# Swapping two early loads, and laying block 1's inputs out in SBUF, in a fused transformer kernel

## The chip, the cores and the metric

The kernel runs on one core of a Trainium2 chip. The metric is the time of one execution on the device in microseconds (us). A kernel is executed several times, and medians are quoted. The profile is taken from one execution; its span, from the first to the last instruction, is about 1.8 us shorter than the time of the same execution.

Names used throughout: x0, x1, x2 are the first tiles of 128 rows of the input (256 KB each). q0 to q3 are the quarters of the weight w1 (512 KB each). PE is the tensor engine, DVE the vector engine, ACT the scalar engine, POOL the GpSimd engine, SP the engine whose queue issues most loads. PT is a tile of transposed probabilities in the attention blocks.

## The reference

Two branches read the same normalised input, and their sum is added to x.

```python
xn = _layernorm(x)
return x + _A_ref(xn, mem0, Wq, Wk, Wv, Wo, seg_len) + _B_ref(xn, w1, w2, w3, w4)

def _B_ref(x, w1, w2, w3, w4):            # x is 2048 x 1024
    h = _gelu(_layernorm(x) @ w1)         # the stage that starts the kernel
    hs = shifted_quarters(h) @ w2
    x1 = x + hs
    return x1 + _gelu(_layernorm(x1) @ w3) @ w4     # inner width 3584

def _A_ref(x, mem0, Wq, Wk, Wv, Wo, seg_len):
    # 64 segments of 32 rows with 8 memory rows, 32 heads of 128:
    # q, k, v, masked softmax, output product; memory goes from segment to segment
    ...
```

## The kernel before

Everything is in bfloat16 with accumulation in float32. The kernel runs branch B first, then all values of branch A (the "V phase"), then branch A's queries, keys, scores and outputs in five blocks of segments ("block 0" to "block 4").

The loads at the start all go through SP's queue:

```python
load_x(0)
load_x(1)
for c in range(4):
    nc.sync.dma_start(w1_sb[:, 2 * c:2 * c + 2, :], w1_v[:, 2 * c:2 * c + 2, :])
    if c == 1:
        load_x(2)
for n in range(3, 7):
    load_x(n)
# ... then w2 and further x tiles
```

The statistics and transposes of the first tiles, and the first product. `stage1_k` does tile 0 one w1 quarter at a time (two values of `k` each), so that PE can start when q0 has landed; `tr(1, ...)` are the transposes of tile 1, which need its normalised rows:

```python
norm_stats(0)
norm_stats(1, 0)          # half of tile 1's statistics
norm2_of(0)               # normalise tile 0
tr(0, 0, True); tr(0, 1, True)
norm_stats(1, 1)          # the other half
...
def stage1_k(xn2T):
    ...
    for k in range(KT):                   # KT = 8
        if k == KT - 2:
            tr(1, 0)
            tr(1, 1)
        for co in range(KT):
            nc.tensor.matmul(...)         # w1_sb[:, k, ...] times tile 0
```

In the V phase the inputs of the blocks are gathered from xT. Those of block 0 stay in SBUF; those of blocks 1 to 4 go through a staging tile to DRAM, and are fetched a block ahead of their use:

```python
if 1 <= hg < 5:
    b, (tl, nb) = hg, tiles_of(hg)
    hTs = abig.tile([P, KT, 464 if b > 2 else 416], BF16, tag="oX", name=f"hTs{b}")
    nc.gpsimd.memset(hTs[:], 0.0)
    fill(hTs, tl, lambda j, b=b: xT[:, j])          # DVE copies
    nc.gpsimd.dma_start(hT_d[b][:], hTs[:].rearrange("p k c -> p (k c)"))
...
if hg == 0:
    tl, nb = tiles_of(0)
    hTb0 = early.tile([P, KT, 416], BF16, tag="hTb0")
    fill(hTb0, tl, lambda j: xT[:, j])
```

```python
def block_setup(b):
    ...
    if b == 0:
        hTb = hTb0
    else:
        hTb = early.tile([P, KT, 464 if b > 2 else 416], BF16, tag=f"hTb{b % 2}")
        nc.gpsimd.dma_start(hTb[:].rearrange("p k c -> p (k c)"), hT_d[b][:])
```

## Time and profile before

| Reading | Before |
|---|---|
| median time, first three runs | 1512.88 us (1511.96 to 1513.14) |
| span of the profile | 1511.0 us |
| PE busy | 1499.8 us, 99% |
| PE waiting, where a cause is named | 3.6 us |
| tile 1's own matmuls begin | 13.57 us |

The page gives the span and the busy time of each engine, with the number of instructions.

```profile
span 1511.0 us, 24305 instructions
...
PE 1499.8 (99%) x9778; PEld 804.0 (53%) x9850; DVE 544.6 (36%) x1136; ACT 504.6 (33%) x1144; POOL 178.9 (12%) x248
```

The kernel is bound by PE nearly everywhere. What can be won by moving loads must therefore be found in PE's waits. The waits view of PE lists who waited for whom: total us, number of times, longest.

```profile
PE ps L307 <- DMA w_sb<-in_B_w_dram: 1.7, 3, 1.0
PE warm L334 <- DVE wz L328: 1.4, 1, 1.4
PE psO L694 <- DMA PT<-Pn: 0.5, 1, 0.5
```

The first line is the start: three waits for quarters of w1. The timeline of PE at the start shows them one by one (start, duration, line, operation, count, and in brackets the idle time just before with its releaser). L307 is tile 0's product, 16 matmuls to a quarter; L294 the transposes; L317 the product of tile 1.

```profile
7.96 1.07 PE L307 MATMUL ps<-xn2T,w_sb 128*128 128x128 bf16 x16 [0.47 <-DMA w_sb<-in_B_w_dram]
9.28 1.07 PE L307 MATMUL ps<-xn2T,w_sb 128*128 128x128 bf16 x16 [0.26 <-DMA w_sb<-in_B_w_dram]
11.32 1.07 PE L307 MATMUL ps<-xn2T,w_sb 128*128 128x128 bf16 x16 [0.97 <-DMA w_sb<-in_B_w_dram]
12.23 0.61 PE L294 MATMUL ps<-c_ident_sb,xn 128*128 128x128 bf16 x8
12.67 1.06 PE L307 MATMUL ps<-xn2T,w_sb 128*128 128x128 bf16 x16
13.57 2.84 PE L317 MATMUL ps<-xn2T,w_sb 128*128 128x128 bf16 x48
```

PE waits for q0, q1 and q2, and from 11.32 us on it is busy. The chain of work that ended last says the same in its first pieces (start, duration, what):

```profile
3.16 8.12 DMA w_sb<-in_B_w_dram
11.28 0.05 issue
11.32 1.07 PE ps L307 x16
```

The landing of q2 is thus the last thing at the start that is not PE's own work. The last two columns of the windows view are the mean busy share of the DMA engines and the rate in GB/s.

```profile
2.00:3.50 1.50, 1.50 (x5) 0.45 (x4) 0.07 (x1) 0.24 (x2) 0.61 (x1) 1.00 0.90 324
3.50:6.50 3.00, 3.00 (x8) 0.87 (x6) 2.69 (x7) 0.00 (x0) 0.72 (x1) 1.00 0.80 226
6.50:9.00 2.50, 2.03 (x25) 1.67 (x24) 1.61 (x5) 1.20 (x4) 1.02 (x4) 1.00 1.05 397
```

There is a dip from 3.5 to 6.5 us: 226 GB/s, against 397 afterwards. For the second half of the change, the same view over the V phase (its third to seventh columns are PE, weight loads, DVE, ACT and POOL), and the loads of block inputs out of DRAM in the view of the tile (count, durations of the issuing instruction in ns, first and last start):

```profile
535.00:756.00 221.00, 219.90 (x1004) 100.14 (x1024) 50.99 (x108) 38.31 (x65) 26.69 (x24) 1.00 0.52 179
```

```profile
L637 POOL DMA_DIRECT2D hTb<-hT_scratch x4: 534/537/558, 646.9 to 1196.1; - x4
```

PE is busy 219.9 of 221 us there; DVE and POOL have ample room. Block 1's load is the one issued at 646.9 us; block 1 itself begins near 870 us.

### The profile page before, as it was taken

What the parts mean: (1) busy time and instruction counts of PE and PEld (TensorE: products, weight loads), DVE (VectorE), ACT (ScalarE), POOL (GpSimd) and SP (SyncE); (2) the same over time, 40 slices, a digit from 0 to 9 for tenths busy, and PEclk for the clock granted to TensorE, in tenths of its full rate; (3) what the DMA queues carried; (4) which work ended last, traced back from release to release, by engine and by line L of the source; (5) the groups of instructions that cost most, each with busy time, mean ns of one, the idle gap of its engine ahead of it and who ended that gap; (6) DMA issues with size and microseconds to landing.
All of it is one profiled execution on the core that took longest, in us unless ns stands there. A gap on an engine that the chain in (4) does not pass through costs nothing.

```text
span 1511.0 us, 24305 instructions
## 1 busy us (share of the span) xinstructions
PE 1499.8 (99%) x9778; PEld 804.0 (53%) x9850; DVE 544.6 (36%) x1136; ACT 504.6 (33%) x1144; POOL 178.9 (12%) x248
## 2 busy tenths in 40 slices
PE   9999999999999999999999999999999999999998
PEld 7844444445444444444456645664665455545555
DVE  8383230100020122222246624661564166516641
ACT  6533203013012011111156614650663266416630
POOL 5231020211111231100000000001000100010001
PEclk9999999999999999999999999999999999999999
DMA  8699752453345887632389957992998299918811
GB/s 292 150 265 315 228 168 89 146 202 104 137 149 151 203 261 258 218 121 82 128 216 257 244 128 171 245 252 69 245 243 206 71 227 224 219 60 199 216 49 51
DMA packets 303539, 274.11 MB, mean 181 GB/s; under 512 B 153926, under 2 KB 270184, under 8 KB 303424
## 3 DMA queue, kind: packets, MB, share of 16 engines
q1 hardware_dynamic: 281248, 189.92, 50.1%
q0 software_dynamic: 22032, 82.54, 15.9%
q8 instruction: 79, 1.29, 0.4%
q14 instruction: 36, 0.29, 0.1%
q10 hardware_dynamic: 144, 0.07, 0.0%
HBM read 190.93 MB, written 46.14 MB: 157 GB/s over the span
## 4 chain that ended last, share of the span: by engine, by line
PE 98%; DMA 1%; issue 0%; SPq 0%; DVE 0%
PE ps L655 30%; PE pso L713 15%; PE ps L594 15%; PE ps L536 13%; PE ps L562 13%; PE ps L394 4%; PE ps L317 3%; PE psO L694 2%; PE psS L670 2%; PE ps L849 1%; PE ps L486 1%; DMA w_sb<-in_B_w_dram 1%; DMA PT<-Pn 1%; PE gps L465 0%; PE ps L451 0%
## 5 line engine op out<-in xcount | busy, mean ns | idle before, releaser
L655 PE MATMUL ps<-hTb,wt 128*128 128x396 bf16 (+2 forms) x2528 | 495.9, 343 | 0.0
L655 PEld LDWEIGHTS <-wt 128*128 128x128 bf16 x2528 | 232.7, 98 | 164.9 <-DMA wt<-in_A_Wq_dram 0.4
L594 PE MATMUL ps<-wt,xT 128*128 128x512 bf16 x1003 | 220.1, 379 | 1.1
L713 PE MATMUL pso<-wo_sb,oX 128*128 128x512 bf16 (+1 forms) x972 | 209.1, 372 | 1.1
L536 PE MATMUL ps<-xn3T,w_sb 128*128 128x512 bf16 x896 | 196.2, 379 | 0.0
L562 PE MATMUL ps<-w_sb,h3T 128*128 128x512 bf16 x873 | 194.3, 379 | 1.2
L594 PEld LDWEIGHTS <-xT 128*128 128x128 bf16 x1024 | 100.1, 98 | 120.9
L537 ACT ACTIVATE h3T<-ps 128x512 bf16<-128x512 f32 x112 | 66.8, 597 | 290.4 <-PE ps L536 289.5
L713 PEld LDWEIGHTS <-oX 128*128 128x128 bf16 x992 | 96.0, 98 | 106.6
L657 ACT CAST KT<-ps 128x462 bf16<-128x462 f32 (+2 forms) x160 | 81.7, 511 | 190.0 <-PE ps L655 185.9
L562 PEld LDWEIGHTS <-h3T 128*128 128x128 bf16 x896 | 86.9, 98 | 103.4
L536 PEld LDWEIGHTS <-w_sb 128*128 128x128 bf16 x896 | 86.5, 98 | 102.1
L676 DVE TENSOR_REDUCE sums<-sm 99x4 f32<-99x396 f32 (+2 forms) x176 | 97.6, 555 | 112.9 <-ACT sm L674 112.9
L659 ACT ACTIVATE QT<-ps 128x462 bf16<-128x462 f32 (+2 forms) x160 | 83.8, 524 | 112.6 <-PE ps L655 98.7
L596 ACT CAST Vs<-ps 128x512 bf16<-128x512 f32 x64 | 37.4, 585 | 233.2 <-PE ps L594 175.0
L672 DVE TENSOR_TENSOR sm<-psS,c_mask_reg_sb 99x396 f32<-99x396 f32 x152 | 86.7, 570 | 74.6 <-PE psS L670 74.5
L674 ACT ACTIVATE sm<-sm 99x396 f32<-99x396 f32 (+2 forms) x176 | 92.7, 527 | 57.7 <-DVE sm L672 53.5
L600 DVE CAST Vs<-ps 128x512 bf16<-128x512 f32 x64 | 44.3, 692 | 170.0 <-PE ps L594 160.4
L682 DVE TENSOR_TENSOR Pn<-sm,rs 99x396 bf16<-99x396 f32 (+2 forms) x176 | 98.9, 562 | 7.2 <-DMA PT<-Pn 1.1
L720 POOL DMA_DIRECT2D out_dram<-ot x30 | 16.4, 545 | 699.4 <-DVE ot L719 693.5
L563 DVE TENSOR_TENSOR R<-ps,R 128x512 f32<-128x512 f32 x32 | 21.9, 690 | 180.1 <-PE ps L562 166.2
L719 DVE TENSOR_TENSOR ot<-pso,Rt 128x512 bf16<-128x512 f32 (+1 forms) x33 | 22.2, 675 | 168.5 <-PE pso L713 164.5
(122 smaller groups left out, 1063.0 us busy)
## 6 DMA issues: line engine op xcount, KB each, us to landing
wt<-in_A_Wq_dram SPq DMA_DIRECT2D x76, 512.0 KB
wt<-in_A_Wk_dram SPq DMA_DIRECT2D x76, 512.0 KB
wt<-in_A_Wv_dram POOLq DMA_DIRECT2D x24, 1024.0 KB, 6.9
V_scratch<-Vs SPq DMA_DIRECT2D x32, 512.0 KB
V<-V_scratch SPq DMA_DIRECT2D x40, 384.0 KB
R_scratch<-x POOLq DMA_DIRECT2D x16, 512.0 KB, 4.0
R<-R_scratch SPq DMA_DIRECT2D x16, 512.0 KB
R_scratch<-R POOLq DMA_DIRECT2D x16, 512.0 KB, 3.1
```

The source lines that it names most:

```text
L536: nc.tensor.matmul(ps[:].rearrange("p (n t) -> p n t", t=P), w3_sb[:, k, f * P:(f + 1) * P], xn3T[tb][:, :, k, :], start=(k == 0), stop=(k ...
L537: nc.scalar.activation(h3T[:, f, :], ps[:], ACTF.Gelu_apprx_tanh)
L562: nc.tensor.matmul(ps[:], h3T[:, f, j * P:(j + 1) * P], w4_sb[:, f, ch * 512:(ch + 1) * 512], start=(f == 0), stop=(f == FT - 1))
L594: nc.tensor.matmul(ps[:], xT[:, m4 * 4 + j, k, :], wv[:, k, :], start=(k == 0), stop=(k == KT - 1))
L655: nc.tensor.matmul(ps[:, :nb], w[:, k, hh * P:(hh + 1) * P], B["hT"][:, k, :nb], start=(k == 0), stop=(k == KT - 1))
L657: nc.scalar.copy(dst[:, hh, :], ps[:, :nb])
L659: nc.scalar.mul(dst[:, hh, :], ps[:, :nb], scale)
L672: nc.vector.tensor_tensor(sm[:T, :, :T], S3, t["mask"][:].unsqueeze(1).to_broadcast((T, 4, T)), op=ALU.add)
L674: nc.scalar.activation(e[:T, :, :T], sm[:T, :, :T], ACTF.Exp, scale=LN2)
L676: nc.vector.tensor_reduce(ss, e[:T, :, :T], axis=AX.X, op=ALU.add)
L682: nc.vector.tensor_tensor(Pn[:T, :, :T], e[:T, :, :T], rs[:T, :].unsqueeze(2).to_broadcast((T, 4, T)), op=ALU.mult)
L713: nc.tensor.matmul(self.ps[:, :self.w], self.oX[0][:, h, self.oX[1] + self.gl * P:self.oX[1] + (self.gl + 1) * P], wo_sb[:, h, self.cc], s ...
```

## The change

Its intent: let PE start on q0 earlier by loading x1 behind q0 rather than ahead of it, and save block 1's inputs the way through DRAM. The place of x2 does not change: it was behind q1 before, and still is. The statistics of tile 1 are no longer cut in halves around tile 0's normalisation.

```diff
                     load_x(0)
-                    load_x(1)
                     for c in range(4):
                         nc.sync.dma_start(w1_sb[:, 2 * c:2 * c + 2, :], w1_v[:, 2 * c:2 * c + 2, :])
-                        if c == 1:
-                            load_x(2)
+                        if c < 2:
+                            load_x(1 + c)
@@
                     norm_stats(0)
-                    norm_stats(1, 0)
                     norm2_of(0)
                     tr(0, 0, True)
                     tr(0, 1, True)
-                    norm_stats(1, 1)
+                    norm_stats(1)
@@
-                if 1 <= hg < 5:
+                if hg < 2:
+                    tl, nb = tiles_of(hg)
+                    hTb01.append(early.tile([P, KT, 416 + 48 * hg], BF16, tag=f"hTb{hg}", name=f"hTb{hg}"))
+                    fill(hTb01[hg], tl, lambda j: xT[:, j])
+                elif hg < 5:
                     b, (tl, nb) = hg, tiles_of(hg)
@@
-            if b == 0:
-                hTb = hTb0
+            if b < 2:
+                hTb = hTb01[b]
             else:
                 hTb = early.tile([P, KT, 464 if b > 2 else 416], BF16, tag=f"hTb{b % 2}")
```

More of the change, by code (lines that the diff above doesn't have):

```diff
@@ L112 @@
     xn_v = xn_d.rearrange("(n p) d -> p n d", p=P)
-    hT_d = {b: tc.dram_tile([P, KT * c], BF16, name=f"hT{b}_scratch") for b, c in ((1, 416), (2, 416), (3, 464), (4, 464))}
+    hT_d = {b: tc.dram_tile([P, KT * c], BF16, name=f"hT{b}_scratch") for b, c in ((2, 416), (3, 464), (4, 464))}
     V_d = tc.dram_tile([S, H * DH], BF16, name="V_scratch")
@@ L580 @@
             wo_sb = abig.tile([P, H, D], BF16)
+            hTb01 = []
             pns = [abig.tile([112, 4, P], BF16, name=f"Pn{i}") for i in range(3)]
@@ L618 @@
                         nc.sync.dma_start(w[:], src[:, :, 512:1024])
-                if hg == 0:
-                    tl, nb = tiles_of(0)
-                    hTb0 = early.tile([P, KT, 416], BF16, tag="hTb0")
-                    fill(hTb0, tl, lambda j: xT[:, j])
             vctx.close()
```

## The prediction

> **What bounds the kernel.** The tensor engine. The page gives PE 1499.8 us busy of a 1511.0 us span (99%), clock 1.000; the chain that ended last is 98% PE. The waits view names 3.6 us of PE waiting: 1.4 at the start (a memset), 1.7 for w1's quarters (three waits, longest 1.0), 0.5 for one PT transpose at 799.4 us. The last 3.8 us (timeline) are the final eviction and store; the other idle time is scattered and looks like missing matmul records. Some 2 us lie where the change could act.
>
> **Part 1, the load order at the start.** Before: x0, x1, q0, q1, x2, q2, q3 on SP's queue (q = quarters of w1). After: x0, q0, x1, q1, x2, q2, q3. x1 (256 KB) and q0 (512 KB) swap; x2 keeps its place. In the timeline, PE starts q0's matmuls at 7.96 (0.47 waiting), q1's at 9.28 (0.26), q2's at 11.32 (0.97), q3's without waiting, and is busy from there; the chain has w1's DMA from 3.16 to 11.28, then only PE.
>
> The Trainium skill ("DMA: Bandwidth & Descriptors", Queues, rings and completion order) says that descriptors on an engine's ring are consumed in order. The trace agrees: these transfers are seen in order of issue. So q0 lands earlier by x1's share: 256 KB at about 390 GB/s (windows, 8 to 11 us), an estimated 0.7 us. PE can use 0.47 of it, as tile 0's transposes end at 7.49. But the bytes ahead of q1 and q2 are the same, so q1 still comes at about 9.28 and q2 at about 11.32; the 0.47 us becomes a longer wait before q1 (about 0.7). Gain on the chain: about 0.
>
> Cost: x1 lands later, near 8.0. Its statistics (twice 0.69, 0.21, 0.22), POOL's power (0.72) and the normalisation (0.55) then give tile 1's rows at about 11.0 instead of 9.3; PE transposes them at 12.2, so about 1 us of slack remains. x2's statistics follow later by 1 to 1.5 us, still before x3 comes (13.3). No loss either.
>
> **Part 2, block 1's inputs.** Removed: one POOL memset (2.90 us), one 832 KB store (about 4 us to landing), one 832 KB load (8.4 us, issued at 646.9). The DVE copies, under 2 us, stay. None is on the chain: the load lands some 200 us before block 1 starts; no PE wait for it is listed. In the V phase (535 to 756 us) PE waits for nothing named, and DVE's evictions wait for PE (2.8 us before each). PE's and ACT's instruction orders are unchanged. Gain: 0 to 0.2 us.
>
> **Prediction.** 1512.4 us, range 1510.8 to 1514.0; before was 1512.88. Chance of faster by over 2% 0.005, within 2% 0.99, slower 0.005. The sum is about -0.2; the other -0.3 is for the PT wait and the DMA dip.
>
> **What would show it.** Right: PE's first w1 matmul near 7.5; q1's wait grown; q2's matmuls still at 11.2 to 11.4; tile 1's transposes without a wait; PE busy within 1 us of 1499.8; three hT stores and loads instead of four. Wrong: q2's matmuls over 0.4 us earlier or later; a new PE wait for tile 1's rows; PE gaps vanishing between 535 and 756 us.
>
> **What would make it wrong.** DMA throughput dips from 3.5 to 6.5 us (139 to 287 GB/s, against 377 before and 410 after; windows). If it depends on the transfers in flight, the swap may move q2 by half a microsecond. A later DMA wait, such as PT's, may also shift.

## The result, and the profile after

| | Before | After |
|---|---|---|
| median of 6 runs each | 1513.01 us (1511.96 to 1513.98) | 1511.46 us (1511.15 to 1512.63) |
| span of the profile | 1511.0 us | 1509.4 us |
| tile 1's own matmuls begin | 13.57 us | 12.03 us |

The ratio is 0.9992, with a 95% interval of 0.9979 to 1.0005. (A ratio is the mean time of one kernel's fast runs over that of the other's of the same rounds, so it is not quite the ratio of the medians quoted.) The page after:

```profile
span 1509.4 us, 24295 instructions
...
PE 1498.9 (99%) x9778; PEld 804.2 (53%) x9850; DVE 544.8 (36%) x1136; ACT 505.2 (33%) x1144; POOL 175.4 (12%) x245
```

POOL is 3.5 us less busy, which is mostly the removed memset. PE's waits after:

```profile
PE warm L333 <- DVE wz L327: 1.4, 1, 1.4
PE psO L693 <- DMA PT<-Pn: 0.6, 2, 0.3
PE ps L306 <- DMA w_sb<-in_B_w_dram: 0.4, 1, 0.4
PE ps L293 <- DVE xn L274: 0.4, 1, 0.4
```

The waits for w1 fell from 1.7 to 0.4 us. PE's timeline at the start after (L306 is tile 0's product, L293 the transposes, L316 tile 1's product):

```profile
7.43 1.95 PE L306 MATMUL ps<-xn2T,w_sb 128*128 128x128 bf16 x32
9.77 1.07 PE L306 MATMUL ps<-xn2T,w_sb 128*128 128x128 bf16 x16 [0.39 <-DMA w_sb<-in_B_w_dram]
10.68 0.61 PE L293 MATMUL ps<-c_ident_sb,xn 128*128 128x128 bf16 x8
11.13 1.07 PE L306 MATMUL ps<-xn2T,w_sb 128*128 128x128 bf16 x16
12.03 2.84 PE L316 MATMUL ps<-xn2T,w_sb 128*128 128x128 bf16 x48
```

PE runs through q0 and q1 without a wait (32 matmuls in one row), and q2 is there at 9.77 instead of 11.32 us. The prediction had said 11.2 to 11.4, and had called a shift of over 0.4 us a sign that it is wrong. The chain and the windows after:

```profile
3.16 6.56 DMA w_sb<-in_B_w_dram
9.73 0.05 issue
9.77 1.07 PE ps L306 x16
```

```profile
2.00:3.50 1.50, 1.50 (x5) 0.47 (x4) 0.02 (x1) 0.24 (x2) 0.61 (x1) 1.00 0.85 235
3.50:6.50 3.00, 2.70 (x8) 0.84 (x6) 2.08 (x6) 0.00 (x0) 0.72 (x1) 1.00 1.03 386
6.50:9.00 2.50, 2.29 (x37) 2.07 (x38) 1.97 (x6) 1.20 (x4) 0.39 (x1) 1.00 1.02 370
```

The dip of 3.5 to 6.5 us is gone; a shorter one now lies before 3.5 us. The V phase and the loads of block inputs after:

```profile
535.00:756.00 221.00, 219.89 (x1006) 100.39 (x1026) 49.46 (x98) 38.96 (x66) 22.75 (x21) 1.00 0.50 171
```

```profile
L636 POOL DMA_DIRECT2D hTb<-hT_scratch x3: 537/537/537, 919.4 to 1194.2; - x3
```

The load at 646.9 us no longer exists, and PE's busy time in the stage is the same to 0.01 us. So the 1.6 us by which the spans differ is, within 0.1 us, the 1.55 us by which q2 came earlier. What is not clear from one pair of profiles is whether the order of loads did that, or chance.

### The profile page after: what moved, and what is told of

It is laid out like the page before. It is cut to its first block, busy times and chain, and to the rows that moved or that the text cites. A ratio compares the mean times of both kernels' runs of the same rounds, so it can differ in the third digit from the quotient of the medians.

```text
span 1509.4 us, 24295 instructions
## 1 busy us (share of the span) xinstructions
PE 1498.9 (99%) x9778; PEld 804.2 (53%) x9850; DVE 544.8 (36%) x1136; ACT 505.2 (33%) x1144; POOL 175.4 (12%) x245
## 4 chain that ended last, share of the span: by engine, by line
PE 98%; DMA 1%; SPq 0%; issue 0%; DVE 0%
PE ps L654 29%; PE pso L712 15%; PE ps L593 15%; PE ps L534 13%; PE ps L560 13%; PE ps L392 4%; PE ps L316 3%; PE psO L693 2%; PE psS L669 2%; DMA PT<-Pn 1%; PE ps L848 1%; PE ps L484 1%; PE gps L463 0%; PE ps L449 0%; DMA w_sb<-in_B_w_dram 0%
```

## The experiments

Timing alone could not decide this, as the first run shows. The readings used below come from the profiles: the moment at which q2's matmuls begin, and the moment at which tile 1's own matmuls begin, after which PE waits little.

### The same two kernels again

`before_again` and `before_third` are the kernel before, unchanged; `after_again` and `after_third` the changed one.

> The kernel before, unchanged, once more. Theory A (the swap itself makes w1's third quarter land earlier): its matmuls start again near 11.3 us, and the early dip in DMA throughput (3.5 to 6.5 us) is there again. Theory B (the dip is chance from execution to execution): that start may fall anywhere between 9.5 and 11.5 us. Time: ratio 1.000 to itself within 0.0005 either way; this is the noise of the comparison.

> The changed kernel once more. Theory A: the third quarter's matmuls start near 9.8 us again, no dip, about 1.2 us faster (ratio 0.9992). Theory B: the start may be anywhere between 9.5 and 11.5 us and the ratio falls towards 1.0.

> The changed kernel a third time, for the comparison with x2_late and to see how often the third quarter comes as early as in its first profile (matmuls at 9.77 us) rather than in its second (10.93). Theory A (the swap always brings it near 9.8): 9.8 again. Theory D (the swap takes the early dip away for good, but the landing of a quarter is set by the slowest of the DMA engines and only 0.3 us come of it in most executions): 10.8 to 11.0, ratio to before 0.9990 to 1.0000.

> The kernel before, a third profile. In three profiles with the old order (two of it, one of part2) 1.03 to 1.13 MB had moved by 6.0 us and the third quarter's matmuls began at 11.0 to 11.3 us; in four with the new order 1.25 to 1.34 MB and 9.8 to 10.9. If the order decides, this one lies in the first group; if chance decides, it may lie in the second.

Timed, `before_again` came out at 0.9993 of the kernel before, interval 0.9977 to 1.0008, where 1.000 within 0.0005 was expected. The comparison of a kernel with itself is thus as far from 1 as the change. (Two of the eleven runs of the kernel before in those rounds, at 1517.5 and 1519.5 us, pull ratios down; the medians suffer less.) The changed kernel's medians were 1512.72 against 1513.24 us, and later 1512.57 against 1513.59: 0.5 and 1.0 us below, after 1.55 at first (ratios 0.9988, interval 0.9973 to 1.0004, and 0.9993, 0.9979 to 1.0007).

The profile of `after_again` at the start:

```profile
8.90 1.07 PE L306 MATMUL ps<-xn2T,w_sb 128*128 128x128 bf16 x16 [0.40 <-DMA w_sb<-in_B_w_dram]
10.93 1.07 PE L306 MATMUL ps<-xn2T,w_sb 128*128 128x128 bf16 x16 [0.96 <-DMA w_sb<-in_B_w_dram]
```

Here PE waits for q1 and q2 nearly as long as before the change, and q2 comes at 10.93. The first profile of the changed kernel was a lucky one. `before_again` had q2 at 11.03, `before_third` at 11.71, `after_third` at 10.55. Theory A in its strong form (always near 9.8) falls. Pure chance (theory B) is made unlikely by the table further down. Theory D's figure (10.8 to 11.0) fits two of the four profiles of the new order; its mechanism, the slowest DMA engine, is looked at below.

### Each half alone

`part1` has the new load and statistics order, with block 1 still through DRAM; `part2` is the reverse. Each is the kernel before with the one half of the diff above. The load order and the order of tile 1's statistics were not separated. But what PE waits for is the landing of q2, and `touch` below has the old order of statistics and yet an early q2.

> The load order and the statistics order alone, block 1 still through DRAM. Theory A: the whole gain, ratio near 0.9992, third quarter's matmuls near 9.8 us. Theory B: ratio near 1.0 and a start that varies. Theory C (the gain in time is block 1's inputs, and the profile's early difference is a coincidence): ratio 1.0.

> Block 1's inputs laid out in SBUF alone, load order as before. Theories A and B: ratio 1.000 within 0.0004, PE busy in the V phase as before, third quarter's matmuls as in the kernel before. Theory C: ratio near 0.9992.

The ratios were 0.9995 (interval 0.9979 to 1.0010) and 0.9993 (0.9977 to 1.0009), medians 1513.52 and 1513.08 beside 1513.24 us: nothing that a timing could tell apart, and `part1` does not show the gain that theory A asked of its time. In the profile `part1` behaves like the changed kernel (q2 at 10.87, tile 1's matmuls from 13.13 us), `part2` like the kernel before (q2 at 11.32, tile 1 from 13.59 us). The V phase and the first block of `part2`:

```profile
535.00:756.00 221.00, 219.90 (x1005) 100.20 (x1024) 49.40 (x98) 38.29 (x65) 22.75 (x21) 1.00 0.51 173
756.00:870.00 114.00, 113.80 (x853) 69.96 (x851) 63.52 (x133) 68.93 (x167) 0.56 (x1) 1.00 0.99 239
```

PE is busy 219.90 us in the V phase, exactly as before. So theory C falls: the half about block 1 removes work from POOL and from DMA, and none that PE waited for.

### Where the time of an execution goes

These are all fourteen profiles. MB are what the DMA engines had moved by 6.0 us (rate of the window from 0 to 6 times its length). "Later waits" are PE's named waits after tile 1 begins: mostly for PT, the transposed probabilities of the attention blocks.

| kernel | first in the queue | MB by 6 us | q2 begins | tile 1 begins | later waits | span | rest |
|---|---|---|---|---|---|---|---|
| before | x0 x1 q0 | 1.05 | 11.32 | 13.57 | 0.5 | 1511.0 | 1496.9 |
| before_again | x0 x1 q0 | 1.13 | 11.03 | 13.30 | 2.2 | 1512.9 | 1497.4 |
| before_third | x0 x1 q0 | 1.15 | 11.71 | 13.97 | 1.0 | 1512.1 | 1497.1 |
| part2 | x0 x1 q0 | 1.03 | 11.32 | 13.59 | 0.5 | 1511.2 | 1497.1 |
| after | x0 q0 x1 | 1.34 | 9.77 | 12.03 | 0.6 | 1509.4 | 1496.8 |
| after_again | x0 q0 x1 | 1.31 | 10.93 | 13.19 | 1.2 | 1511.3 | 1496.9 |
| after_third | x0 q0 x1 | 1.25 | 10.55 | 12.79 | 0.4 | 1510.0 | 1496.8 |
| part1 | x0 q0 x1 | 1.32 | 10.87 | 13.13 | 1.2 | 1511.6 | 1497.3 |
| half_swap | x0 half q0 x1 | 1.15 | 10.69 | 12.96 | 0.3 | 1509.8 | 1496.5 |
| touch | x0 touch x1 q0 | 1.16 | 10.73 | 12.97 | 1.6 | 1511.4 | 1496.8 |
| gate | x0 q0 x1 | 1.33 | 10.42 | 12.66 | 2.1 | 1512.5 | 1497.7 |
| x2_late | x0 q0 x1 | 1.35 | no wait | 12.47 | 1.1 | 1510.7 | 1497.1 |
| x12_late | x0 q0 q1 | 1.37 | no wait | 13.72 | 1.0 | 1511.5 | 1496.8 |
| x2_last | x0 q0 x1 | 1.25 | 9.84 | 12.09 | 0.4 | 1509.9 | 1497.4 |

"Rest" is the span less the two columns before it (start of tile 1 and later waits). It lies between 1496.5 and 1497.7 us in all fourteen profiles. So most of what sets one execution of these kernels apart from another is two things: when the start is over, and how long PE later waits, above all for PT. (The 1.2 us over which the rest varies is not explained.) The second varied from 0.4 to 2.2 us between executions of unchanged kernels. That is why timings of unlike kernels overlap.

Compare the four profiles of the old order (first four rows) with the four of the new (next four). Tile 1 begins at 13.30 to 13.97 us in the one group, mean 13.61, and at 12.03 to 13.19 in the other, mean 12.79. The groups do not overlap (were the order without effect, four against four would fall this way in one of 70 cases), and the means differ by 0.8 us. The bytes moved by 6 us do not overlap either (1.03 to 1.15 against 1.25 to 1.34 MB). So the order does take the dip away, and is worth about 0.8 us on average; the other 0.7 us of the first pair of profiles was the luck of that execution. The size is rough. The profiles come from several calls (on chips 8, 0 and 14 by the record; for the first pair it names none), and in the one call that profiled both orders (chip 8) the difference is 0.3 us: 13.30 and 13.59 against 13.19 and 13.13. The three median differences of the changed kernel, 1.55, 0.5 and 1.0 us, agree with a gain of this order; that of `part1` does not, since its median lay 0.3 us above the kernel before.

### Does the number of bytes ahead set q2's landing?

`x2_late` moves x2 behind q2, `x12_late` moves both x1 and x2 behind it; `gate` holds all loads behind q3 until tile 1's rows are normalised, so that nothing later competes with the quarters.

```diff
-                        if c < 2:
-                            load_x(1 + c)
+                        if c in (0, 2):              # x2_late
+                            load_x(1 + c // 2)
```

```diff
-                        if c < 2:
-                            load_x(1 + c)
+                        if c == 2:                   # x12_late
+                            load_x(1)
+                            load_x(2)
```

```diff
+                    def later_loads():               # gate; called after norm2_of(1)
+                        nc.sync.dma_start(gate_d[:], xn2s[1][0:1, 0:64])
+                        # ... x3 to x6, w2, x7 to x9 as before
```

> The changed kernel with the third x tile behind w1's third quarter instead of its second. If the bytes ahead of the third quarter set its landing, 256 KB fewer at about 390 GB/s bring its matmuls 0.67 us earlier than in the changed kernel of this call, near 10.2, and the time falls by about 0.5 us below it. If another thing sets it (stalls of single DMA engines in the first microseconds, whatever the order), less than 0.2 us comes of it. The statistics of tile 2 must not delay PE: its transposes start without a wait.

> Both x tiles behind the third quarter. The quarter's matmuls at the earliest time yet if bytes set it, about 1.3 us earlier than in the changed kernel (but not before the second quarter's are done). In exchange tile 1's rows come late: they were ready at 9.9 us with x1 second, and the transposes for them need x1's landing plus about 3 us. PE should now wait 1.5 to 3 us for DVE there, and the whole be slower by 0.5 to 2 us.

> The changed kernel with all loads behind w1's fourth quarter held until tile 1's normalised rows exist (a 128-byte store of them goes first in the queue), so that nothing later competes with the quarters. If the third quarter is held up by later transfers on faster DMA engines, its matmuls start earlier than 10.4 us. If its slowest engine is late by its own early stalls, the start stays at 10.8 to 11.0 as in most profiles of the changed kernel. The time itself may grow, since the fourth x tile comes later.

The starts of `x2_late`, then of `x12_late`:

```profile
7.56 3.04 PE L306 MATMUL ps<-xn2T,w_sb 128*128 128x128 bf16 x48
10.43 0.61 PE L293 MATMUL ps<-c_ident_sb,xn 128*128 128x128 bf16 x8
11.56 1.07 PE L306 MATMUL ps<-xn2T,w_sb 128*128 128x128 bf16 x16 [0.52 <-DMA w_sb<-in_B_w_dram]
```

```profile
7.65 2.84 PE L307 MATMUL ps<-xn2T,w_sb 128*128 128x128 bf16 x48
12.37 0.62 PE L294 MATMUL ps<-c_ident_sb,xn 128*128 128x128 bf16 x8 [1.88 <-DVE xn L275]
```

In `x2_late` 48 matmuls run in one row: q2's begin without a listed wait, near 9.5 us (two thirds into that row), some 1 us earlier than in `after_third` and more than the 0.67 us expected. The bytes ahead do count, though single profiles overlap: the first one of the changed kernel had q2 at 9.77 us with all of them ahead. But q3, which still has the same bytes ahead of it, now makes PE wait 0.52 us, so of that 1 us only 0.3 reaches tile 1 (12.47 against 12.79). The timed gain over the changed kernel did not show (median 1512.87 beside 1512.57 us). `x12_late` shows the price of a late x1: PE waits 1.88 us for tile 1's rows, in the expected range of 1.5 to 3, and tile 1 begins 0.9 us later than in `after_third`. x1 can stand behind q0, and not behind q2. (`x12_late` and `gate` were executed once each for time, 1513.22 and 1514.31 us, and so were `before_third`, `half_swap` and `touch`, 1513.95, 1511.57 and 1513.17 us; with the spread shown above that says nothing.)

In `gate` q2's matmuls begin at 10.42 us, inside the changed kernel's 9.8 to 10.9 and between the two marks of the expectation (before 10.4, or 10.8 to 11.0). One profile can't exclude a small effect of later transfers, but q2 is held back without them too.

A side reading: in the kernel before, 2.36 MB stand in the queue up to and including q2 (three x tiles and three quarters). By 11.32 us, when q2 was seen, the engines had moved 3.10 MB. So much of what came behind q2 had overtaken its last pieces. The Trainium skill says why that can be ("DMA: Bandwidth & Descriptors", section "Why a DMA increments its semaphore by 16 and not by 1"): a transfer runs on up to 16 engines that finish independently, and it counts as landed when the last has finished.

The traces agree, and show more. Each of these loads reports by 16 increments of its semaphore, whose times the packed traces keep. No view of the profile prints them. They don't say which engine an increment is from. A "part" below is what one increment reports; a "late" part is over 0.5 us behind the transfer's median.

| kernel | q0: first to last part | q2: first part | q2: median | q2: last part | late parts of q2 |
|---|---|---|---|---|---|
| before | 5.37 to 7.91 | 9.47 | 9.92 | 11.28 | 3 |
| before_again | 5.43 to 7.64 | 9.23 | 9.66 | 10.98 | 4 |
| before_third | 5.26 to 8.09 | 9.46 | 9.87 | 11.67 | 5 |
| part2 | 5.49 to 7.92 | 9.25 | 9.75 | 11.27 | 6 |
| after | 4.73 to 5.16 | 9.09 | 9.20 | 9.73 | 1 |
| after_again | 4.64 to 5.13 | 9.05 | 9.35 | 10.88 | 2 |
| after_third | 4.75 to 5.37 | 9.08 | 9.53 | 10.50 | 1 |
| part1 | 4.64 to 5.16 | 9.15 | 9.42 | 10.83 | 2 |
| gate | 4.74 to 5.21 | 9.08 | 9.22 | 10.37 | 1 |

In all nine profiles PE starts q2 0.04 to 0.05 us after the last part. Between the four profiles of the old order and the four of the new, q2's first part moves by 0.26 us on average and its last by 0.81. So two thirds of the gain is that the last parts lag less behind the first, and where q2 comes late in the new order, one or two late parts hold it. In `gate` fifteen parts are there by 9.57 us and the last at 10.37, with nothing behind q3 to compete. In the kernel before, first and last part are 1.85 us apart for q1 and still 1.80 for q2 and 1.81 for q3, as if the same engines stayed behind; that they are the same ones is not shown.

### Why does the dip go?

Two edits try to separate "w1 is read early" from "a larger transfer stands second". `half_swap` cuts q0 in two halves of 256 KB around x1. `touch` is the kernel before with a read of 64 bytes from each of the 256 rows of q0 ahead of x1.

```diff
-                    for c in range(4):
+                    nc.sync.dma_start(w1_sb[:, 0:1, :], w1_v[:, 0:1, :])      # half_swap
+                    load_x(1)
+                    nc.sync.dma_start(w1_sb[:, 1:2, :], w1_v[:, 1:2, :])
+                    for c in range(1, 4):
```

```diff
                     load_x(0)
+                    touch = big.tile([P, 2, 32], BF16)                        # touch
+                    nc.sync.dma_start(touch[:], w1_v[:, 0:2, 0:32])
                     load_x(1)
```

> The changed kernel with w1's first quarter in two halves of 256 KB, one before the second x tile, one after it, so that what stands second in the queue has the size of an x tile but comes from w1. If it is which tensor is read second that takes the dip away, 1.25 MB or more are moved by 6.0 us, as in the changed kernel. If it is that a larger transfer stands second, the dip is back (1.03 to 1.13 MB).

> The kernel before with one small read more, 64 bytes from each of the 256 rows of w1's first quarter, between the first and the second x tile. If the dip is the price of first reads of w1, and an early touch of it pays that price beside x's transfers, 1.2 MB or more are moved by 6.0 us and the third quarter's matmuls begin before 11.0 us. If not, the start stays at 11.0 to 11.6 us and the dip remains.

The windows of 3.5 to 6.5 us, of `half_swap` and then of `touch`:

```profile
3.50:6.50 3.00, 3.00 (x8) 0.89 (x6) 2.08 (x6) 0.00 (x0) 0.72 (x1) 1.00 0.84 274
```

```profile
3.50:6.50 3.00, 3.00 (x8) 0.90 (x6) 2.55 (x6) 0.00 (x0) 0.72 (x1) 1.00 0.98 314
```

Both lie between the old order (218 to 259 GB/s in four profiles) and the new (350 to 386). Both moved 1.15 or 1.16 MB by 6 us: neither of the values that the expectations named, and no more than `before_third` (1.15). Yet both have q2 at 10.7 us like the new order, with no wait for q0 or q1. So the bytes moved by 6 us, a mean over the engines, do not set q2's landing; its last part does, at 10.65 and 10.69 us, 1.04 and 1.24 us behind the first. What the profiles do show is a regularity: wherever a read of w1 stands ahead of x1 in the queue, even one of 16 KB, q2's matmuls begin before 11.0 us (ten profiles, three of them with fewer bytes ahead of q2), and wherever none does, after it (four). The gap is narrow, 10.93 against 11.03 us. That first reads of w1 are slow, and are better paid early, is an idea that could fit this; but `touch` missed one of the two marks set for it and is one profile, and where all of q0 stands second its sixteen parts land within 0.32 to 0.62 us of one another (eight profiles), against 2.21 to 2.83 us where it stands third, behind x1 (the four of the old order). Why engines fall behind there, and with it the cause of the dip, stays open. (`touch` also had a wait of 1.4 us for a later weight, in the product with w3 on line 538, that no other profile has; its span is the worse for it.)

### A further version

`x2_last` moves x2 behind q3, to free q3 as well.

```diff
-                        if c < 2:
-                            load_x(1 + c)
+                        if c in (0, 3):
+                            load_x(1 + c // 3)
```

> The changed kernel with the third x tile behind w1's fourth quarter. With it behind the third quarter, PE no longer waited for the third but 0.5 us for the fourth. Now the fourth has 256 KB fewer ahead of it as well: PE should begin tile 1's own matmuls near 11.8 to 12.0 us (before: 13.3 to 13.6). Against that stand tile 2's statistics, which come later: PE may wait up to 0.6 us for its rows. Time 0.7 to 1.3 us below the kernel before.

Tile 1 begins at 12.09 us, against the 11.8 to 12.0 expected. But the chain now goes through x2 and its statistics:

```profile
3.68 8.13 DMA xt<-in_A_x_dram
...
11.84 0.69 DVE st L259
...
13.71 0.73 POOL rr L265
...
14.46 0.56 DVE xn L274
...
15.07 0.40 PE ps L293 x4
```

PE's transposes of tile 2 start at 15.07 us, 2.98 us after tile 1's matmuls begin; in the changed kernel's first profile it was 2.68 us (14.71 less 12.03). So 0.3 us of the gain is given back there. The median was 1511.68 beside 1512.47 us, 0.8 us less than before, ratio 0.9994 (0.9981 to 1.0008). That is as much as the changed kernel's 0.5 to 1.55, and no more. The expected gain of 0.7 to 1.3 us was met, but it has not been shown to beat the changed kernel. Between landing of w1 and readiness of the x tiles, little is left at the start.

## Why the prediction was right or wrong

- **The time and the verdict were right.** 1512.4 us was predicted with 1510.8 to 1514.0; 1511.46 was measured, within 2%. The reading behind it holds: PE is 99% busy, and only some 2 us lay where the change could act.
- **Part 2 was right.** No gain was expected from block 1's inputs, 0 to 0.2 us. `part2` has the same PE time in the V phase (219.90 us) and the same start, and its rest in the table is like the others'. One store and one load fewer were seen.
- **q0 was right for PE, not in its landing.** PE's first w1 matmul came at 7.43 us (predicted near 7.5), its wait gone. But q0 was estimated to land 0.7 us earlier by x1's share of the bytes, and it landed at 5.16 instead of 7.91 us. PE could use no more of it, as tile 0's transposes came first.
- **The step that failed** is "the bytes ahead of q1 and q2 are the same, so q1 still comes at about 9.28 and q2 at about 11.32 ... Gain on the chain: about 0". The bytes were the same; when the last of 16 engines had moved its share of them was not. In four profiles of the new order q2 came at 9.77 to 10.93 us, in four of the old at 11.03 to 11.71. The term put at 0 measured about 0.8 us on average, and 1.55 in the profile that came with the result. Of the 0.8 us, 0.26 is that q2's first part came earlier and the rest that its last part lagged less: 3 to 6 late parts in the old order, 1 or 2 in the new. Why the order does that was not found. The closing paragraph had named the dip as the thing that could do this, "by half a microsecond", and had then left it out of the sum but for a lean of 0.3 us shared with PT.
- **q1's longer wait was wrong.** It was to grow to about 0.7 us. It was 0.40 in two of the four profiles of the new order, and absent in two.
- **The cost side was about right.** Tile 1's rows were predicted at about 11.0 us. They were ready at 9.9 in the first profile (the normalisation starts at 9.35 and takes 0.55), where x1's statistics began at 6.76 us without waiting for x1; in the other three of the new order they waited 0.33 to 0.75 us for x1, and the rows were ready at 10.3 to 10.8. No PE wait came of it, as predicted. `x12_late` shows that the slack is real and finite.
- **The lean towards a shorter PT wait** had no ground: that wait was 0.4 to 1.2 us in the four profiles of the new order, and 0.5 to 2.2 in the four of the old.

So the total came out inside the range while the term that moved was one that the sum had at zero: the range, 3.2 us wide, was kept, and the reasoning for the start was not.

## What to carry to other kernels

When loads at the start of a kernel are reordered, counting the bytes ahead of a transfer gives the order of landings but not their times: here the same bytes moved at 226 or at 386 GB/s from 3.5 to 6.5 us in the first pair of profiles. What the waiting engine sees is the last of a transfer's 16 parts, in the kernel before 1.8 us behind the first. A gain of half a thousandth is below what a handful of timings can show; take several profiles of each version and compare the moment at which the critical engine gets going. Splitting a span into start, named waits and a constant rest tells quickly which part an edit has touched, and traffic taken off a stage in which the critical engine never waits gives no time back.

## What the Trainium skill lacked or had wrong

- "DMA: Bandwidth & Descriptors", section "Queues, rings and completion order": it tells the order in which descriptors are consumed, and the transfers were seen in that order. It does not say that the rate in the first microseconds depends on the order of tensors in the queue: 218 to 259 GB/s from 3.5 to 6.5 us with x0, x1 first, 350 to 386 with x0, q0 first (four profiles each).
- The same page, section "Where 436 GB/s comes from", has about 358 GB/s binding for transfers from HBM into SBUF. Read alone it misleads for a program on one core: 397 GB/s were moved from 6.5 to 9 us in the kernel before, reading x and w1 from HBM. The page's table of measurements with one core, which reaches 425, fits better, and the note under it calls about 358 the share of each when both cores of a memory domain stream.
- No page gives how far the parts of one load drift apart at the start of a kernel: first and last part of q2 were 1.75 to 2.21 us apart in the old order and 0.63 to 1.83 in the new (four profiles each).
- No page gives the spread of waits for small DMA transposes between executions of one kernel: the waits for PT summed to 0.5, 2.2 and 1.0 us in three profiles of the same code.
